# Writing the constant rows of four stacked operands on ScalarE instead of VectorE

## The chip, the cores and the metric

The kernel runs on one core of a Trainium2 chip. A core has TensorE (PE in the profile; its weight loads are shown as PEld), VectorE (DVE), ScalarE (ACT), GpSimd (POOL) and SyncE (SP), and each works through its own list of instructions in a fixed order. The metric is the device time of one execution in microseconds (us); less is better.

## The reference

Clustered attention feeds a routed mixture of experts, which feeds a dense layer pair with the mish activation:

```python
# 2 batches, 8 heads, 768 tokens, head size 64, 16 clusters
q_assign = argmax(normalize(q) @ normalize(centroids).T)   # k_assign alike
mask = q_assign[:, :, :, None] == k_assign[:, :, None, :]
scores = where(mask, scale * (q @ k.T), -1e9)
attn = exp(scores - scores.max(-1)); attn /= attn.sum(-1) + 1e-9
x = (attn @ v) as 1536 rows of 512
# 8 experts, one for each row: logits = x @ w_gate + modality_bias[modality_id]
x[e] = gate_w[e] * (relu(x[e] @ w1[e]) @ w2[e])
h = x @ w_in; g = h * tanh(softplus(h)); out = g @ w_out
```

## The kernel before, in words

There are 16 attention problems (2 batches of 8 heads). For each, the operands of the score product lie in one of four stacks, `QK[0]` to `QK[3]`, used in turn. A stack is a tile of 128 partitions and four planes (QA, QB, KA, KB) of 768 half-precision numbers. Partitions 0 to 95 hold high and low parts of q and k and arrive by four DMAs that `stack(i)` (L258 to L261) issues from SP's queue out of `hl`, where `split_pair` (L245 on ScalarE, L249 on VectorE or GpSimd) has put the high and the low part of a pair of heads. Partitions 96 to 127 carry the mask: in QA and KA the cluster of each token, written once for each head (L303, and for head 0 L332 and L334), in QB the running row maximum (L378, two of the rows), and in KB a constant that never changes: 65504 in partitions 96 and 97 and zero elsewhere. `shift_rows` writes the zeros of QB (L151, GpSimd) and then the constant rows of KB (L153), once for each of the four stacks. The constant comes from `frow`, a column that GpSimd builds (L146, L148).

At the start, the list of work is this. Four loads bring q and k of the first two pairs of heads; a fifth, from ScalarE's queue, brings the centroids `cen`. VectorE and ScalarE compute the norms of the centroids (L165 to L170, and in `centroid_stacks` two rounds of L175 to L177, then L178 and L179), VectorE scales the centroids (L181, L182), PE transposes them (L184, L185) and VectorE writes them as `CC` (L186 to L190). With `CC`, PE can compute the similarity of tokens and clusters, for head 0 from `hl` (L313) and for head 1 from its stack (L273). VectorE turns them into one-hot rows (L319 to L325, L286 to L292), and these go into the stacks. Then the scores of head 0 start: L350 and L355 for the row maxima, L391 for the scores themselves. `load_v` (L202) brings v of batch 0, which ScalarE scales (L221) before the split of v. ScalarE also copies the one-hot rows of head 1 (L301), which SP then sends into the stack (L303).

The function of the program that calls `shift_rows` asks for the rows of stack 0 early and for those of stacks 1 to 3 as steps that are interleaved with the main loop. The order that is written into each engine's list, though, is not this order: a planner puts the instructions of every engine but SP in order by its own estimate of times, and keeps dependencies. SP's list stays as written in the program. Each engine then follows its list and waits on semaphores.

After attention for batch 0 the expert phase begins to interleave with attention (`moe1`, L1007 and its neighbours), the weights of the dense layers are converted by VectorE and ScalarE (L1027 to L1035), and the dense layers follow (L1103 to L1164).

Of the kernel before, what the change touches and what calls it, by code (L numbers as in the profile page):

```python
# [13 lines left out]
AF = mybir.ActivationFunctionType  # L14
ALU = mybir.AluOpType
# [9 lines left out]
def clustered_attention_moe_kernel(  # L25
# [16 lines left out]
    nc = tc.nc  # L42
# [100 lines left out]
    QA, QB, KA, KB = range(4)  # L143
    QK = [ap.tile([P, 4, S], F16, name=f"QK{i}") for i in range(NST)]
    frow = ap.tile([P, 1], F32, name="frow")
# [4 lines left out]
    def shift_rows(i, eng):  # L150
        eng.memset(QK[i][96:128, QB, :], 0.0)  # L151
        yield
        nc.vector.tensor_scalar(out=QK[i][96:128, KB, :], in0=QK[i][96:128, QB, :], scalar1=frow[96:128], scalar2=None, op0=ALU.add)  # L153
        yield

    cen = a3.tile([P, S], F32, tag="e32", name="cen")[:, 0:P]
# [333 lines left out]
    def attention():  # L490
# [81 lines left out]
        assign_first()  # L572
        load_v(0, 0, T)
        run(shift_rows(0, nc.gpsimd))
        sk, sq = split_pair(1, 1, True), split_pair(1, 0, True)
        next(sk)
# [24 lines left out]
        for k_ in range(1, NST):  # L601
            put(start(shift_rows(k_, nc.gpsimd), 1), 1)
# [765 lines left out]
```

## Time and profile before

| | us |
|---|---|
| median of 3 runs | 689.66 |
| the three runs | 689.56, 689.66, 696.43 |
| the profiled execution | 697.58 |
| its span, first to last instruction | 695.9 |
| mean granted TensorE clock in it | 0.971 of full speed |

The profiled execution is one of its own, 7.92 us above the median, and 1.68 us of it lie outside the span. Rows of its trace give a start and a duration in us from the start of the span; in the timeline, brackets hold the time that the engine sat idle before the instruction and what released it.

### The profile page before, as it was taken

How to read it: one execution, taken by the hardware profiler on the slowest of the kernel's cores; microseconds unless marked ns; L12 is line 12 of the kernel's file. 1: busy time of each engine (PE TensorE's matmuls, PEld its weight loads, DVE VectorE, ACT ScalarE, POOL GpSimd, SP SyncE). 2: the span in 40 equal slices, each digit the busy share in tenths (PEclk: the TensorE clock that was granted, in tenths of full speed). 3: DMA queues.
4: the chain of work that ended last, by engine and by line, in shares of the span. 5: the costliest groups of instructions: out<-in, count | busy, mean ns of one | idle time of the engine just before them, and what ended most of it. 6: DMA issues, size and time to landing. Idle time of an engine off the chain costs nothing.

```text
span 695.9 us, 14026 instructions
## 1 busy us (share of the span) xinstructions
PE 616.7 (89%) x5618; PEld 409.6 (59%) x5619; DVE 400.6 (58%) x751; ACT 459.3 (66%) x699; POOL 294.9 (42%) x251
## 2 busy tenths in 40 slices
PE   1698999987589988987999889999999999999995
PEld 1365867756356645554766556666666667667542
DVE  6768767689699899999858888823121110110100
ACT  2587998875678767765677678846554476776500
POOL 5577888796776744551141211111311212313211
PEclk9999999989789999999999999999999999999999
DMA  7532372312853234346445544321100000000000
GB/s 229 139 74 64 87 206 53 87 41 61 273 162 102 68 97 121 123 128 189 135 158 183 183 150 161 113 61 31 47 16 1 15 16 1 31 1 31 2 31 34
DMA packets 56743, 64.43 MB, mean 93 GB/s; under 512 B 10080, under 2 KB 46944, under 8 KB 56672
## 3 DMA queue, kind: packets, MB, share of 16 engines
q1 hardware_dynamic: 42064, 48.74, 24.1%
q10 hardware_dynamic: 12688, 8.42, 4.0%
q0 software_dynamic: 1920, 6.32, 2.4%
q8 instruction: 46, 0.75, 0.5%
q14 instruction: 25, 0.20, 0.1%
HBM read 46.23 MB, written 6.32 MB: 76 GB/s over the span
## 4 chain that ended last, share of the span: by engine, by line
PE 40%; DVE 28%; issue 10%; ACT 9%; DMA 7%; SPq 3%; POOL 1%; ACTq 0%; POOLq 0%; DVEq 0%
PE h L1007 12%; PE o L1159 12%; PE eps L1007 6%; DVE f L1028 4%; DVE mxh L351 3%; DVE f L1030 3%; PE s L391 2%; DVE w L922 2%; DMA QK<-hl 2%; DVE f L1027 2%; DMA QK<-oT 2%; DVE win L1035 2%; DVE mxh L356 1%; DVE dg L702 1%; PE eps L273 1%
## 5 line engine op out<-in xcount | busy, mean ns | idle before, releaser
L114 POOL TENSOR_TENSOR el<-e,eh 128x768 f16<-128x768 f32 x86 | 146.0, 1709 | 63.9 <-ACT eh L400 42.9
L1007 PE MATMUL h<-x,win 128*128 128x256 f16 x1152 | 133.3, 273 | 3.2 <-ACT s L1103 2.4
L1007 PEld LDWEIGHTS <-win 128*128 128x128 f16 x1152 | 112.5, 98 | 24.1 <-issue 4.7
L1110 DVE SCALAR_TENSOR_TENSOR s<-s,h 128x1024 f32<-128x1024 f32 x24 | 29.3, 1222 | 167.4 <-ACT s L1108 164.8
L1007 PEld LDWEIGHTS <-w 128*128 128x128 f16 x768 | 75.2, 99 | 67.6 <-issue 12.1
L114 POOL TENSOR_TENSOR xb<-s,xb 128x1024 f16<-128x1024 f32 x18 | 39.6, 2201 | 142.7 <-ACT xb L1113 142.5
L1159 PE MATMUL o<-wout,xb 128*128 128x512 f16 x432 | 96.8, 379 | 0.0
L391 PE MATMUL s<-QK 128*128 128x384 f16 x320 | 80.2, 346 | 9.6 <-ACT e L393 9.2
L393 ACT ACTIVATE e<-s 128x384 f32<-128x384 f32 x152 | 70.0, 489 | 24.5 <-PE s L391 19.3
L1007 PE MATMUL eps<-xw,w 128*128 128x416 f16 x384 | 76.8, 349 | 8.7 <-DVE hT L969 3.2
L400 ACT ACTIVATE eh<-e 128x768 f16<-128x768 f32 x88 | 74.3, 848 | 2.5 <-PE s L391 1.3
L351 DVE TENSOR_REDUCE mxh<-x 128x1 f32<-128x512 f32 x96 | 64.6, 680 | 17.2 <-PE x L350 17.1
L1103 ACT ACTIVATE s<-h,cst 128x512 f32<-128x512 f32 x48 | 32.8, 686 | 61.8 <-PE h L1007 61.5
L1007 PE MATMUL eps<-hT,w 128*128 128x416 f16 x384 | 71.6, 339 | 0.7 <-DVE hT L969 0.7
L1159 PEld LDWEIGHTS <-xb 128*128 128x128 f16 x432 | 42.3, 98 | 47.6
L429 PE MATMUL av<-vst,el 128*128 128x65 f16 x528 | 61.3, 197 | 5.8 <-POOL el L114 5.8
L427 PE MATMUL av<-vst,eh 128*128 128x65 f16 x528 | 63.8, 198 | 1.9 <-DVE xt L442 1.6
L428 PE MATMUL av<-vst,eh 128*128 128x64 f16 x528 | 63.8, 199 | 0.0
L429 PEld LDWEIGHTS <-el 128*128 128x128 f16 x528 | 51.3, 102 | 15.5 <-POOL el L114 11.3
L427 PEld LDWEIGHTS <-eh 128*128 128x128 f16 x528 | 51.5, 100 | 9.1 <-DVE xt L442 2.6
L391 PEld LDWEIGHTS <-QK 128*128 128x128 f16 x384 | 35.3, 103 | 33.3 <-issue 20.6
L428 PEld LDWEIGHTS <-eh 128*128 128x128 f16 x528 | 51.4, 101 | 3.3 <-issue 0.3
(224 smaller groups left out, 1053.4 us busy)
## 6 DMA issues: line engine op xcount, KB each, us to landing
wf<-in_moe_w_dram ACTq DMA_DIRECT2D x16, 512.0 KB
raw<-in_moe_w_in_dram SPq DMA_DIRECT2D x16, 512.0 KB
raw<-in_moe_w_out_dram SPq DMA_DIRECT2D x16, 512.0 KB
wf<-in_moe_w_dram SPq DMA_DIRECT2D x16, 512.0 KB
QK<-hl SPq DMA_DIRECT2D x32, 192.0 KB
xs<-dr SPq DMA_DIRECT2D x12, 258.0 KB
t<-in_k_dram SPq DMA_DIRECT2D x8, 384.0 KB
t<-in_q_dram SPq DMA_DIRECT2D x8, 384.0 KB
```

The lines of the kernel that those rows point to most:

```text
L114: nc.gpsimd.tensor_tensor(out=out_, in0=in0, in1=in1, op=ALU.subtract)
L351: nc.vector.reduce_max(out=mx_t[i][:, t, 0:1], in_=sp, axis=AX.X)
L391: nc.tensor.matmul(sps[hf][:, 0:HS], lhsT=st[:, KA + a, kt * P:(kt + 1) * P], rhs=st[:, QA + a, hf * HS:(hf + 1) * HS], start=(a == 0), st ...
L393: nc.scalar.activation(out=e32[:, hf * HS:(hf + 1) * HS], in_=sps[hf][:, 0:HS], func=AF.Exp, scale=1.0 / float(D) ** 0.5)
L400: nc.scalar.activation(out=eh, in_=e32, func=AF.Copy)
L427: nc.tensor.matmul(av[:, t, :], lhsT=eh[:, cols], rhs=vs[:, h, 0:NV], start=(kt == 0 and t == 0), stop=False, skip_group_check=True)
L428: nc.tensor.matmul(av[:, t, 0:D], lhsT=eh[:, cols], rhs=vs[:, h, NV:], start=False, stop=False, skip_group_check=True)
L429: nc.tensor.matmul(av[:, t, :], lhsT=el[:, cols], rhs=vs[:, h, 0:NV], start=False, stop=(kt == T - 1), skip_group_check=True)
L1007: nc.tensor.matmul(out_, lhsT=wc[:, a, kk, ms], rhs=mv[:, c, kk, :], start=(i == 0), stop=(i == n - 1))
L1103: nc.scalar.activation(out=s[:, u:u + hf], in_=pt[:, u:u + hf], func=AF.Sigmoid, scale=2.0 ** -17, bias=cst[:, 1:2])
L1110: nc.vector.scalar_tensor_tensor(out=s, in0=s, scalar=2.0 ** -6, in1=pt, op0=ALU.mult, op1=ALU.mult)
L1159: nc.tensor.matmul(pts[t], lhsT=gsl[q % 2][f // FB][:, f % FB, a, t * P:(t + 1) * P], rhs=wout[:, c, f, :], start=(f == 0 and i_ == 0), st ...
```

## The change

The constant rows of each stack are no longer written by a VectorE `tensor_scalar` that adds `frow` to the zero rows, but by a ScalarE activation (Identity) with the same zero rows as input and `frow` as bias for each partition. There are four such instructions, 32 partitions by 768 half-precision numbers each.

```diff
     def shift_rows(i, eng):
         eng.memset(QK[i][96:128, QB, :], 0.0)
         yield
-        nc.vector.tensor_scalar(out=QK[i][96:128, KB, :], in0=QK[i][96:128, QB, :], scalar1=frow[96:128], scalar2=None, op0=ALU.add)
+        nc.scalar.activation(out=QK[i][96:128, KB, :], in_=QK[i][96:128, QB, :], func=AF.Identity, bias=frow[96:128])
         yield
```

## Rows read from the trace of the kernel before

**Rows 1.** The page's head: busy time of each engine.

```profile
PE 616.7 (89%) x5618; PEld 409.6 (59%) x5619; DVE 400.6 (58%) x751; ACT 459.3 (66%) x699; POOL 294.9 (42%) x251
```

**Rows 2.** Busy time by stretch; last columns: granted clock, DMA share, GB/s.

```profile
140.00:340.00 200.00, 165.51 (x1902) 110.35 (x1902) 182.87 (x331) 139.65 (x248) 117.34 (x90) 0.93 0.43 128
340.00:696.00 356.00, 340.00 (x2255) 217.16 (x2251) 120.84 (x198) 214.82 (x255) 75.42 (x50) 0.99 0.19 63
```

**Rows 3.** The chain that ended last, 7 to 25 us: start, duration, what.

```profile
7.33 4.01 DVE QK L153 x4
...
12.82 0.26 DVE cen L182
...
24.92 0.74 ACT oT L301
```

**Rows 4.** The four constant-row writes by line: duration in ns, min/median/max.

```profile
L153 DVE TENSOR_SCALAR QK<-QK,frow x4: 413/1016/1790, 7.3 to 10.9; 32x768 f16<-32x768 f16 x4
```

**Rows 5.** Timeline of GpSimd, 6 to 11 us.

```profile
6.24 0.18 POOL L148 TENSOR_SCALAR_AFFINE_SELECT frow<-frow 128x1 f32<-128x1 f32 x1
...
7.09 1.64 POOL L249 TENSOR_TENSOR hl<-t,hl 128x768 f16<-128x768 f32 x1 [0.67 <-ACT hl L245]
8.69 1.75 POOL L249 TENSOR_TENSOR hl<-t,hl 128x768 f16<-128x768 f32 x1
```

**Rows 6.** Timeline of VectorE, 7 to 13 us.

```profile
7.16 0.14 DVE L177 TENSOR_SCALAR cs<-cs 128x1 f32<-128x1 f32 x1
...
11.56 0.22 DVE L176 SCALAR_TENSOR_TENSOR cs<-cs 128x1 f32<-128x1 f32 x1
...
12.39 0.39 DVE L181 TENSOR_SCALAR cen<-cen,cs 128x32 f32<-128x32 f32 x2
```

**Rows 7.** Timeline of VectorE and GpSimd, later in attention.

```profile
166.75 1.64 POOL L114 TENSOR_TENSOR el<-e,eh 128x768 f16<-128x768 f32 x1 [0.43 <-PE av L429]
167.19 1.24 DVE L755 TENSOR_SCALAR gg<-gg 128x6 f32<-128x6 f32 x1
174.75 1.65 POOL L114 TENSOR_TENSOR el<-e,eh 128x768 f16<-128x768 f32 x1 [1.67 <-ACT eh L400]
174.92 1.50 DVE L810 SCALAR_TENSOR_TENSOR tab<-ge,gst 128x8 f32<-128x8 f32 x1
```

**Rows 8.** Timeline of ScalarE, 5 to 22 us.

```profile
5.41 2.54 ACT L245 ACTIVATE hl<-t 128x768 f16<-128x768 f32 x3
20.34 0.80 ACT L332 ACTIVATE QK<-x 32x768 f16<-32x768 f16 x1 [12.38 <-PE x L330]
21.16 1.15 ACT L221 ACTIVATE vf<-vf 128x512 f32<-128x512 f32 x2
```

**Rows 9.** Groups of ScalarE by shape: count, busy us, mean ns, idle before.

```profile
L1103 ACT ACTIVATE s<-h,cst 128x512 f32<-128x512 f32 x48 | 32.8, 686 | 61.8 <-PE h L1007 61.5
L1103 ACT ACT_TABLE_LOAD x24 | 30.8, 1283 | 2.5 <-PE h L1007 2.0
```

**Rows 10.** Timeline of PE, 15 to 25 us: similarities of heads 1 and 2.

```profile
15.88 1.26 PE L273 MATMUL eps<-CC,QK 96*128 96x16 f16 x24
23.84 0.85 PE L273 MATMUL eps<-CC,QK 96*128 96x16 f16 x15
```

**Rows 11.** DMA packets in 13.2:13.6, 18.5:19.0, 19.8:20.0 and 21.5:22 us, in that order.

```profile
DMA packets 15, 0.03 MB, mean 77 GB/s; under 512 B 0, under 2 KB 0, under 8 KB 15
DMA packets 67, 0.12 MB, mean 236 GB/s; under 512 B 11, under 2 KB 37, under 8 KB 67
DMA packets 31, 0.04 MB, mean 200 GB/s; under 512 B 6, under 2 KB 30, under 8 KB 31
DMA packets 7, 0.01 MB, mean 12 GB/s; under 512 B 3, under 2 KB 7, under 8 KB 7
```

**Rows 12.** Timeline of SP's queue: an issue of stack 0, the one of v.

```profile
6.66 0.66 SPq L259 DMA_DIRECT2D QK<-hl  x1
11.43 0.59 SPq L202 DMA_DIRECT2D vf<-in_v_dram  x1
```

## What the change should do to the time: the prediction

> **What bounds the kernel now.** I read the page first: PE is the busiest engine at 89% of the span, but no engine is full [rows 1]. The table by stretch says where each limit holds: between 140 and 340 us VectorE is busy 182.87 of 200 us and PE 165.51, and after 340 us PE is busy 340 of 356 us, ScalarE and VectorE far less [rows 2]. Neither stretch contains the changed instructions. They run once, early, so the third view is the chain of waits over the first 25 us. There all four constant-row writes stand on the chain, back to back, 4.01 us from 7.33 us on, between two rounds of the centroid norm: the norm goes on only when they end, at 11.34, and the scaled centroids that PE waits for are ready at 12.82 + 0.26 = 13.08 [rows 3]. The planner has hoisted all four of them in front of work that everything later needs. Whatever the start loses is lost for the whole kernel, because the loads of later heads, the expert phase and the dense layers are all released by work of the start; only the first loads run by themselves. So the question is how much of 4.01 us the start gives back.
>
> **What is removed.** The four writes took 413, 1016 and 1790 ns (least, median, longest) though their shape is the same [rows 4]. The timeline of GpSimd explains it: its two subtractions of the second pair run from 7.09 to 8.73 and from 8.69 to 10.44 [rows 5]. The first write starts at 7.33 and waits for the end of the first subtraction, the second for the end of the second; only the last two run at their own pace of 0.41 us. Thus 4 x 0.41 = 1.65 us are work and some 2.4 us are waiting for GpSimd. The waiting needn't go with the writes. What stands behind them on VectorE is the rest of the chain: L175, L176, L177, L178, L179, then two L181 and one L182, and some of these can be held in the same way. Later rows show which kinds: a `tensor_scalar` of 128x6 took 1.24 us and ended at 168.43 where GpSimd's subtraction ended at 168.39, and an L810 of the operation that L176 is took 1.50 us and ended at 176.42, GpSimd's at 176.40 [rows 7]. A 128x1 `tensor_scalar` such as L177 was not held: 0.14 us, within GpSimd's first subtraction [rows 5, 6].
>
> Sum for the new start. L175 (0.16 us) begins at 7.33 and L176 is due at 7.53. If it is held to 8.73, then L181, which begins 12.39 - 11.56 = 0.83 us after L176 [rows 6], is due at 9.56 and is held to 10.44. Held instructions ended 0.03 to 0.22 us behind GpSimd (the 0.22 is the first write's, 7.33 + 1.62 to 8.73), so the first L181 ends at 10.47 to 10.66. It ended at 12.39 + 0.24 = 12.63 before, and the scaled centroids came 0.45 us later; now they come at 10.9 to 11.1 instead of 13.08: 2.0 to 2.2 us gained. If L176, which has only one element in each partition, is not held, L181 is due at 7.53 + 0.83 = 8.36, the first one waits to 8.73, the second to 10.44, and the gain is 2.3 us. Either way the second subtraction stands in the path. If neither were held, the gain would be the whole 4.01 us.
>
> The Trainium skill has a rule for this that speaks against the change: its page "SBUF — State Buffer", section "SBUF: two separate sides", says that VectorE and GpSimd share one pair of ports as an exclusive lock, taken for the whole instruction, by a VectorE operation with two SBUF inputs or in a two-port mode against a GpSimd operation that reads SBUF. By that rule L176 is held as well, and the sum would be the lower one, 2.0 to 2.2 us; the rows of L755 and L810 agree with it [rows 7].
>
> **What of it reaches the end.** Next come PE's L313, then L273 for head 1, then VectorE's chain and ScalarE's L332. L273 began at 15.88 [rows 10] and needs stack 1 in place. Stack 1's short packets were over by 13.2 us, where only the 2 KB packets of v are left [rows 11], so a start at 13.8 is covered. L332 moves from 20.34 to about 18.2 and ends at 19.0. Behind it in ScalarE's order stands L221, which began at 21.16 [rows 8] and needs v. This load hides: it was issued at 11.43 [rows 12], nothing of the change moves that, and its last packets fall between 18.6 and 20.0 us (of the packets over 2 KB, some of which are stack 2's, 30 are left in 18.5 to 19.0 and one in 19.8 to 20.0) [rows 11]. So L221 can begin between 19.0 and 20.0, a gain of 1.2 to 2.1 us, and with it L301 at 24.92, which the chain passes through [rows 3]. Stack 2 is the other thing that becomes late: its last packets came after 21.5 us [rows 11], and head 2's similarities, at 23.84 in PE's order [rows 10], would move to about 21.8, when it has just landed. I take 1.8 us, with v complete at 19.4, the middle of its window.
>
> **What is added.** Four activations on ScalarE. The nearest row is L332 with the same shape and no bias, 0.80 us [rows 8]; the nearest with a bias for each partition is L1103, 686 ns for 512 elements, which scales to 1.03 us for 768 [rows 9]. So 3.2 to 4.1 us in all; I take 3.5, nearer to the same shape. ScalarE finishes its splits at 5.41 + 2.54 = 7.95 and sits idle for 12.38 us before L332 [rows 8]; about 10.2 us of that remain after the gain, and the rows are wanted only by the scores of head 0, past 20 us. So I cost them at nothing. If Identity made ScalarE load another table and the old one again, two loads of 1283 ns [rows 9] add 2.6 us, still under the cover. Without cover the price is 3.2 to 4.1 us of ScalarE, in front of whatever the planner puts behind them. No DMA is added or moved, and nothing waits on a new semaphore but ScalarE, for GpSimd's `frow`, done at 6.24 + 0.18 = 6.42 us [rows 5].
>
> **The sum.** The profiled execution would go from 697.58 to 695.8 us, its span from 695.9 to 694.1. That execution lies 7.92 us above the median of 689.66, which is nearer to what will be measured: 689.66 - 1.8 = 687.9 us, 0.3% less. About 1%, 6.9 us, is what a measurement of this kernel can tell from no change, since the three runs of the same program differ by 6.87 us.
>
> **Rivals.**
> *The whole 4.01 us* come back: 685.7. For it: the writes stand on the chain with all of it. Against it: the hold by GpSimd, then v and stack 2. It needs another order, with the splits of the second pair later. 7%.
> *Nothing:* the planner uses the freed slot for other VectorE work, such as a step of later heads, or v is what the start waits for. 689 to 690.5. 12%.
> *Slower, by ScalarE's order.* The four activations are put ahead of a split of the first pair. They can't start before `frow` is done at 6.4 us, so the split of q that began at 5.4 [rows 8] would begin at 6.4 + 3.2 = 9.6, 4.2 us later; SP's L259 waits for it, and every issue behind that in SP's list, v among them, moves from 6.66 to about 10.4, 3.7 us [rows 12]. v then lands past 22.7 us and L221 starts there instead of at 21.16: 1.5 to 2.5 us slower, 691.7. It decides from the point at which a constant row stands ahead of the second split in ScalarE's list. Against it: ScalarE has 12 free microseconds behind the splits. If they are put behind L332 instead, about 3.5 - 1.8 = 1.7 us are lost in front of L221, the same size. 10%.
> *The rest of the program falls elsewhere.* The planner orders four engines, and it has already carried these writes across the whole start; a start that is 1.8 us shorter can change orders later. And the granted clock, 0.93 of full speed between 140 and 340 us [rows 2], means that about 0.07 x 200 / 0.5 = 28 us of that stretch ran at the lower of PE's two clock levels, 1.2 GHz; the same program came out at 689.56 and at 696.43. I price this by that spread, 6.9 us to either side: 681 us with 16%, 695 to 698 us with 13%.
>
> **How the numbers follow.** The forecast itself, 687.6 to 688.5, has 42%. Faster by over 1% (under 682.8) comes from the last rival alone, 0.16. Slower by over 1% (over 696.6) from its other side, 0.13. The rest, 0.71, is within 1%: forecast, whole gain, nothing, and ScalarE's order. For 8 in 10 the range must go into both outer cases without holding them: 682 to 696.
>
> **What would show each step.** In the new trace no constant row stands on VectorE; four activations of 0.8 to 1.0 us stand on ScalarE between 7.9 and 18 us; L176 or an L181 is longer than 1 us while GpSimd subtracts; L182 ends at 10.8 to 11.1; L332 starts at 18 to 18.5; L221 starts at 19.0 to 20.0; the later stretches keep their order, 1.8 us earlier. The prediction is wrong if L182 comes before 10 us and the gain is carried on, if constant rows stand ahead of a split or right behind L332, or if the order of work in the stretch from 140 to 340 us is another.

## The result, and the profile of the changed kernel

| | before | changed |
|---|---|---|
| median of 19 runs each, us | 694.57 | 689.32 |
| lowest and highest, us | 688.81 to 698.62 | 683.86 to 696.07 |
| ratio | 1 | 0.9919, 95% interval 0.9893 to 0.9944 |
| profiled execution and span, us | 697.58, 695.9 | 687.57, 685.9 |
| mean granted clock in it | 0.971 | 0.975 |

The changed kernel is 0.8% faster: (1 - 0.9919) x 694.57 = 5.6 us, between 3.9 and 7.4. The ratio leaves out three disturbed runs of the changed kernel (695.69 to 696.07 us); the medians are those of all runs, and by them the gain is 694.57 - 689.32 = 5.25 us. The time forecast, 687.9 us, and the sign are right, the size of the change is not: 1.8 us were forecast from a base of 689.66 us, and 19 runs put that base at 694.57. The three runs shown in advance were a low draw, and that the time came out right is luck.

The start goes much as forecast, with two differences. The page's busy times say only that the writes moved: VectorE 395.8 us for 400.6, ScalarE 462.3 for 459.3 [rows 1].

```profile
PE 613.6 (89%) x5618; PEld 408.7 (60%) x5619; DVE 395.8 (58%) x747; ACT 462.3 (67%) x703; POOL 298.0 (43%) x251
```

The timeline of VectorE, 7.3 to 10.3 us (start, duration, what), answers to [rows 6]:

```profile
7.36 0.16 DVE L175 RECIPROCAL cs<-cs 128x1 f32<-128x1 f32 x1
7.56 1.38 DVE L176 SCALAR_TENSOR_TENSOR cs<-cs 128x1 f32<-128x1 f32 x1
...
9.54 0.39 DVE L181 TENSOR_SCALAR cen<-cen,cs 128x32 f32<-128x32 f32 x2
9.97 0.26 DVE L182 TENSOR_SCALAR cen<-cen,cs 128x64 f32<-128x64 f32 x1
```

and that of GpSimd to [rows 5]:

```profile
7.28 1.64 POOL L249 TENSOR_TENSOR hl<-t,hl 128x768 f16<-128x768 f32 x1 [0.86 <-ACT hl L245]
11.57 1.64 POOL L249 TENSOR_TENSOR hl<-t,hl 128x768 f16<-128x768 f32 x1 [2.65 <-ACT hl L245]
```

L176 took 1.38 us for 0.22 and ended at 8.94, GpSimd's subtraction at 8.92: held, as forecast. L175, a reciprocal of one input just ahead of it, went through beside GpSimd in 0.16 us. The two L181 took their 0.39 us and were not held, because the second subtraction didn't run beside them. It came at 11.57, after a wait for ScalarE. So L182 ended at 10.23, 2.85 us earlier than the 13.08 of before, not 2.0 to 2.2.

Why the second subtraction came late stands in the timeline of ScalarE, 7 to 25 us [rows 8]:

```profile
7.23 3.40 ACT L153 ACTIVATE QK<-QK,frow 32x768 f16<-32x768 f16 x4
10.65 0.84 ACT L245 ACTIVATE hl<-t 128x768 f16<-128x768 f32 x1
18.04 0.80 ACT L332 ACTIVATE QK<-x 32x768 f16<-32x768 f16 x1 [6.55 <-PE x L330]
20.55 1.15 ACT L221 ACTIVATE vf<-vf 128x512 f32<-128x512 f32 x2 [1.71 <-DMA vf<-in_v_dram]
...
23.69 0.85 ACT L301 ACTIVATE oT<-oC 128x384 f16<-128x384 f16 x1
```

The planner put the four writes ahead of the fourth split, not behind it. They take 3.40 us together, 0.85 from one to the next, with no table load between them. L332 starts at 18.04, 2.30 us earlier. Then ScalarE sits idle for 1.71 us, waiting for v, and L221 starts only 0.61 us earlier than the 21.16 of before. The chain of waits says the same: it is v, not VectorE, that ends the start now [rows 3]. Ahead of v it runs through SP's queue, where the issues of the stacks, back to back from 6.04 us on, stand in front of v's.

```profile
11.46 9.08 DMA vf<-in_v_dram
...
23.78 0.76 ACT oT L301
```

The issue of v is at its old place [rows 12], and it lands at 20.53. The packets of 20.0:20.2, 20.2:20.4 and 20.4:20.6 us show how late its large ones run (the last two figures are the packets under 2 KB and under 8 KB; their difference, 4, 3 and 0, is the packets over 2 KB):

```profile
DMA packets 31, 0.05 MB, mean 230 GB/s; under 512 B 5, under 2 KB 27, under 8 KB 31
DMA packets 25, 0.03 MB, mean 169 GB/s; under 512 B 6, under 2 KB 22, under 8 KB 25
DMA packets 28, 0.04 MB, mean 184 GB/s; under 512 B 4, under 2 KB 28, under 8 KB 28
```

Stacks 1 and 2 have become late too. In the timeline of PE, both heads' similarities now wait for a DMA of their stack, where before there was no wait [rows 10]. For stack 1 this is what turns the 2.85 us of L182 into the 2.30 of L332:

```profile
13.61 1.24 PE L273 MATMUL eps<-CC,QK 96*128 96x16 f16 x23 [0.28 <-DMA QK<-hl]
...
22.67 0.21 PE L273 MATMUL eps<-CC,QK 96*128 96x16 f16 x1 [0.83 <-DMA QK<-hl]
```

Of L301's gain of 1.13 us (24.82 to 23.69), 0.61 is L221's; the other 0.52 is an L222 that stood ahead of L301 and now stands behind it. That is a change of order, and it isn't the only one. From about 21 us to 450 us the lists of PE, VectorE, ScalarE and GpSimd are rearranged throughout: in PE's list, 5,571 instructions as it was recorded for the experiments below, 2,679 places hold another instruction, and a line-by-line comparison takes out or puts in 1,188. SP's list is the same. So the span's 10.0 us needn't come from the start. L440 runs once at the end of each of the 16 heads; its group, heads 0 to 6 and heads 7 to 15 (first and last start at the end of the row), of the kernel before:

```profile
L440 DVE TENSOR_SCALAR r<-av x7: 152/154/165, 54.7 to 133.1; 128x6 f32<-128x6 f32 x7
L440 DVE TENSOR_SCALAR r<-av x9: 149/152/157, 149.9 to 318.5; 128x6 f32<-128x6 f32 x9
```

and of the changed kernel:

```profile
L440 DVE TENSOR_SCALAR r<-av x7: 150/165/167, 51.6 to 132.0; 128x6 f32<-128x6 f32 x7
L440 DVE TENSOR_SCALAR r<-av x9: 147/151/165, 145.3 to 311.1; 128x6 f32<-128x6 f32 x9
```

The lead is 3.1 us at head 0, 1.1 at head 6, 4.6 at head 7 and 7.4 at head 15. A gain of the start that is handed on would stay what it is. The stretch from 140 to 340 us and the one after it answer to [rows 2] (columns as there):

```profile
140.00:340.00 200.00, 167.85 (x1935) 113.02 (x1934) 184.77 (x361) 143.74 (x251) 120.27 (x87) 0.95 0.45 131
340.00:686.00 346.00, 328.75 (x2174) 209.43 (x2172) 113.88 (x162) 207.18 (x247) 72.28 (x47) 0.99 0.19 63
```

In the 200 us every engine did slightly more work than before, VectorE 184.77 us for 182.87 and PE 167.85 for 165.51, and the granted clock was 0.95 for 0.93. No one resource stands out.

### The profile page after: what moved, and what is told of

Read it like the earlier page. It is cut to its first block, busy times and chain, and to the rows that moved or that the text cites. A ratio compares the mean times of both kernels' runs of the same rounds, so it can differ in the third digit from the quotient of the medians.

```text
span 685.9 us, 14017 instructions
## 1 busy us (share of the span) xinstructions
PE 613.6 (89%) x5618; PEld 408.7 (60%) x5619; DVE 395.8 (58%) x747; ACT 462.3 (67%) x703; POOL 298.0 (43%) x251
## 4 chain that ended last, share of the span: by engine, by line
PE 44%; DVE 23%; issue 10%; DMA 9%; ACT 9%; SPq 3%; POOL 1%; ACTq 0%; POOLq 0%; DVEq 0%
PE h L1007 13%; PE o L1159 12%; PE eps L1007 7%; DMA QK<-hl 3%; DVE f L1028 3%; DVE mxh L351 3%; PE s L391 3%; DVE f L1030 2%; DMA raw<-in_moe_w_out_dram 2%; DVE w L922 2%; DVE f L1027 2%; DVE win L1035 2%; DMA vf<-in_v_dram 1%; PE x L350 1%; PE av L425 1%
## 5 line engine op out<-in xcount | busy, mean ns | idle before, releaser
L114 POOL TENSOR_TENSOR el<-e,eh 128x768 f16<-128x768 f32 x86 | 149.5, 1750 | 53.2 <-ACT eh L400 39.8
L393 ACT ACTIVATE e<-s 128x384 f32<-128x384 f32 x152 | 69.1, 489 | 20.0 <-PE s L391 18.5
L1007 PE MATMUL eps<-xw,w 128*128 128x416 f16 x384 | 72.9, 339 | 4.9 <-DVE hT L969 3.4
```

What stands on the lines that cost most here:

```text
L114: nc.gpsimd.tensor_tensor(out=out_, in0=in0, in1=in1, op=ALU.subtract)
L393: nc.scalar.activation(out=e32[:, hf * HS:(hf + 1) * HS], in_=sps[hf][:, 0:HS], func=AF.Exp, scale=1.0 / float(D) ** 0.5)
L1007: nc.tensor.matmul(out_, lhsT=wc[:, a, kk, ms], rhs=mv[:, c, kk, :], start=(i == 0), stop=(i == n - 1))
```

## The experiments

Three theories. *Start:* the time comes back in the first 25 us, as forecast, whichever engine the writes leave VectorE's early place for. *Order:* most of it comes from the new lists that the planner made, and would come with the writes left where they were. *Engine:* it matters that ScalarE has the writes and VectorE hasn't.

To tell them apart, the order has to be held still while the writes move. In most kernels below each engine's list is therefore recorded from one planned program and fixed by dependencies that the planner obeys and that leave no instruction and no semaphore behind. Only a loop over leftover blocks, which isn't entered, can come out in another order. In the traces a and c run the four engines' instructions in before's order, the writes apart, and b in the changed kernel's. No kernel leaves out or changes part of the computation.

```diff
-        clustered_attention_moe_kernel(tc, *args)
+        clustered_attention_moe_kernel(tc, *args); _pin(tc, nc)
...
+            if prev is not None:
+                tc.add_manual_dep(nc.get_inst_by_name(f"I-{at}"), f"I-{prev}", info, reason="the recorded order")
```

All were timed in five rounds, on three chips. Ratios are to the kernel before on the same chip, whose medians there were 693.18, 693.15 and 693.95 us.

| kernel | writes on | lists | median us (runs) | ratio, 95% interval |
|---|---|---|---|---|
| a_act_old_order | ScalarE | before's | 691.96 (12) | 0.9972, 0.9942 to 1.0002 |
| b_dve_new_order | VectorE, old place | changed kernel's | 687.02 (6) | 0.9896, 0.9859 to 0.9933 |
| b2_dve_new_order | the same again | | 686.73 (11) | 0.9901, 0.9871 to 0.9930 |
| c_dve_late | VectorE, later | before's | 692.47 (12) | 0.9977, 0.9947 to 1.0006 |
| d_act_l301 | ScalarE | before's, L301 earlier | 690.89 (12) | 0.9956, 0.9929 to 0.9983 |
| h1_new_to128 | VectorE, old place | changed to 128 us, then before's | 691.02 (12) | 0.9961, 0.9932 to 0.9990 |
| h2_new_from128 | VectorE, old place | before's to 128 us, then changed | 689.70 (12) | 0.9960, 0.9927 to 0.9993 |
| f_new_l301 | ScalarE | changed, L301 earlier | 687.70 (12) | 0.9923, 0.9891 to 0.9955 |
| after_again | ScalarE | changed kernel as it is | 690.27 (12) | 0.9931, 0.9899 to 0.9964 |
| o_third_order | VectorE, old place | a third plan | 693.59 (12) | 0.9994, 0.9968 to 1.0021 |
| o_fourth_order | VectorE, old place | a fourth plan | 696.73 (12) | 1.0034, 1.0005 to 1.0062 |
| pool_writes | GpSimd | planner's own | 701.58 (7) | 1.0108, 1.0068 to 1.0148 |

**a_act_old_order: the edit alone.** The writes are on ScalarE at the place that the changed kernel gives them; every list is before's otherwise.

```diff
-        nc.vector.tensor_scalar(out=QK[i][96:128, KB, :], in0=QK[i][96:128, QB, :], scalar1=frow[96:128], scalar2=None, op0=ALU.add)
+        nc.scalar.activation(out=QK[i][96:128, KB, :], in_=QK[i][96:128, QB, :], func=AF.Identity, bias=frow[96:128])
```

> The four constant-row writes are on ScalarE, ahead of the last split as in the changed kernel, and every other instruction of every engine keeps the order of the kernel before. Start path plus new order (my theory): the start gains about 2.3 us up to L332, v holds L221 so that the gain behind it is 0.6 to 1.1 us, and the kernel is 0.5 to 2.5 us faster than before (ratio 0.9965 to 0.999). Start path alone: the whole of the measured 5.6 us is here, ratio about 0.992. New order alone: no change, ratio 1.000 within 0.0015.

Measured 0.9972: 1.9 us, with an interval from 4.0 faster to 0.1 slower. Its timeline of ScalarE:

```profile
18.05 0.80 ACT L332 ACTIVATE QK<-x 32x768 f16<-32x768 f16 x1 [6.73 <-PE x L330]
20.48 1.15 ACT L221 ACTIVATE vf<-vf 128x512 f32<-128x512 f32 x2 [1.63 <-DMA vf<-in_v_dram]
...
23.62 0.62 ACT L222 ACTIVATE vst<-vf 128x512 f16<-128x512 f32 x1
24.14 0.86 ACT L301 ACTIVATE oT<-oC 128x384 f16<-128x384 f16 x1
```

and its L440, heads 0 to 6 and 7 to 15:

```profile
L440 DVE TENSOR_SCALAR r<-av x7: 149/155/164, 54.1 to 132.3; 128x6 f32<-128x6 f32 x7
L440 DVE TENSOR_SCALAR r<-av x9: 148/151/165, 149.3 to 317.2; 128x6 f32<-128x6 f32 x9
```

L332 gains 2.29 us, v takes all but 0.68 of it away, and this remainder is handed on (the L222 ahead of L301, which the changed kernel has behind it, stands where it stood): 0.6, 0.8, 0.6 and 1.3 us at heads 0, 6, 7 and 15. This is what the edit does by itself in this order. The ratio alone doesn't show it, since its interval includes no gain, and two traces of one program can lie further apart (b and b2, next).

**b_dve_new_order and its repeat b2_dve_new_order: the order alone.** The writes stay on VectorE, at their old place behind L177; every list is the changed kernel's otherwise. Against the changed kernel:

```diff
-        nc.scalar.activation(out=QK[i][96:128, KB, :], in_=QK[i][96:128, QB, :], func=AF.Identity, bias=frow[96:128])
+        nc.vector.tensor_scalar(out=QK[i][96:128, KB, :], in0=QK[i][96:128, QB, :], scalar1=frow[96:128], scalar2=None, op0=ALU.add)
```

> The four writes stay on VectorE at their old place between the two norm rounds, and every other instruction of every engine has the order of the changed kernel. Start path plus new order: the norm ends at 13.1 us as before, and the kernel is 3 to 5 us faster than before (ratio 0.993 to 0.996). Start path alone: no change, 1.000 within 0.0015. New order alone: 0.992.

> The changed kernel's order with the writes left on VectorE, once more, since it had 6 runs and gave 0.9896. If the start's 2 us add to the order's gain, this must come out slower than the changed kernel (0.9919 and 0.9931): 0.994 to 0.997. If the new order has no use for a start that is earlier by 2 us: 0.990 to 0.993.

Measured 0.9896 and 0.9901: about 7 us, with nothing of the edit in it. The timeline of ScalarE of the first shows that the start is as late as before:

```profile
20.64 0.80 ACT L332 ACTIVATE QK<-x 32x768 f16<-32x768 f16 x1 [12.37 <-PE x L330]
...
24.61 0.85 ACT L301 ACTIVATE oT<-oC 128x384 f16<-128x384 f16 x1
```

and L440 that the lead comes after it:

```profile
L440 DVE TENSOR_SCALAR r<-av x7: 150/165/166, 53.6 to 132.7; 128x6 f32<-128x6 f32 x7
L440 DVE TENSOR_SCALAR r<-av x9: 147/150/165, 146.0 to 310.5; 128x6 f32<-128x6 f32 x9
```

The lead over the kernel before is 1.1 us at head 0, 0.4 at head 6, 3.9 at head 7 and 8.0 at head 15. The trace of b2, the same program, has

```profile
L440 DVE TENSOR_SCALAR r<-av x7: 152/165/167, 51.8 to 129.5; 128x6 f32<-128x6 f32 x7
L440 DVE TENSOR_SCALAR r<-av x9: 146/149/165, 142.8 to 306.9; 128x6 f32<-128x6 f32 x9
```

a lead of 2.9, 3.6, 7.1 and 11.6 us. Two executions of one program thus lie 1.8 us apart at head 0 and 3.6 at head 15, and a difference of that size between two traces shows nothing by itself. The changed kernel, with the better start and the same lists, is 2.0 us ahead of b at head 0 and 0.6 behind at head 15, and 0.2 ahead of b2 and 4.2 behind. The theory of the order stands, on the ratios; start and engine don't explain the result. The gain is larger than the 0.993 to 0.996 expected if start and order share it, and as large as the order alone was to give.

**c_dve_late: another place on the same engine.** In before's lists two of the writes go behind L182 and two behind the first L292.

```diff
 L177 TENSOR_SCALAR cs<-cs 128x1
-L153 TENSOR_SCALAR QK_117<-QK_117,frow 32x768
-L153 TENSOR_SCALAR QK_118<-QK_118,frow 32x768
-L153 TENSOR_SCALAR QK_119<-QK_119,frow 32x768
-L153 TENSOR_SCALAR QK_120<-QK_120,frow 32x768
...
 L182 TENSOR_SCALAR cen<-cen,cs 128x64
+L153 TENSOR_SCALAR QK_117<-QK_117,frow 32x768
+L153 TENSOR_SCALAR QK_118<-QK_118,frow 32x768
...
```

> The four writes stay on VectorE but later in its list, two behind L182 and two behind the first L292, where VectorE waits for PE; every other instruction keeps the order of the kernel before. If it is the place of the writes that costs and not their engine, L176 is held to 8.7 to 9.0 us, an L181 to 10.4 to 10.7, L182 ends at 10.9 to 11.1, and the kernel changes as much as with the writes on ScalarE in the old order (0.5 to 2.5 us faster by my theory). If VectorE's load as such counts, less than half of that.

Measured 0.9977, as a, and as there the interval includes no gain. In the traces the two come out alike, too: L221 waits for v in both and starts at 20.41 here, 0.75 us earlier than before, and at 20.48 in a. So nothing speaks for the engine, but v hides what difference there may be: L182 gains 1.94 us here (13.08 to 11.14) and 2.85 in the changed kernel. This kernel also keeps GpSimd's two subtractions back to back, 7.45 to 10.68 us, so its timeline of VectorE shows the second hold that the prediction had:

```profile
7.65 1.45 DVE L176 SCALAR_TENSOR_TENSOR cs<-cs 128x1 f32<-128x1 f32 x1
...
9.71 1.15 DVE L181 TENSOR_SCALAR cen<-cen,cs 128x32 f32<-128x32 f32 x2
10.89 0.25 DVE L182 TENSOR_SCALAR cen<-cen,cs 128x64 f32<-128x64 f32 x1
11.18 0.76 DVE L153 TENSOR_SCALAR QK<-QK,frow 32x768 f16<-32x768 f16 x2
```

The two L181 take 1.15 us for 0.39, and L182 ends at 11.14. The writes, held by nobody here, take 0.76 us for two.

**d_act_l301: v's wait taken out of L301's way.** As a, with L301 ahead of L221 in ScalarE's list.

```diff
 L332 ACTIVATE QK_117<-x 32x768
+L301 ACTIVATE oT<-oC 128x384
 L221 ACTIVATE vf<-vf 128x512 x2
...
-L301 ACTIVATE oT<-oC 128x384
```

> As the first kernel of this group (writes on ScalarE, old order), and in ScalarE's list the copy of head 1's one-hot rows, L301, moved ahead of the scaling of v, L221. If the load of v, through L221 in front of L301, is what stops the gain, L301 starts at about 20 instead of 24 us, SP's L303 with it, and the kernel is 1.5 to 4 us faster than the first kernel of this group. If something else is late next (stack 2, PE's row maxima), it is within 0.7 us of it.

Measured 0.9956: 3.0 us, between 1.2 and 4.9. The timeline of ScalarE, where L301 now goes at 20.23, and L221 behind it finds v there:

```profile
20.23 0.85 ACT L301 ACTIVATE oT<-oC 128x384 f16<-128x384 f16 x1 [1.30 <-DVE oC L299]
20.98 1.13 ACT L221 ACTIVATE vf<-vf 128x512 f32<-128x512 f32 x2
```

Its L440:

```profile
L440 DVE TENSOR_SCALAR r<-av x7: 149/155/165, 51.7 to 130.0; 128x6 f32<-128x6 f32 x7
L440 DVE TENSOR_SCALAR r<-av x9: 148/151/165, 145.9 to 314.1; 128x6 f32<-128x6 f32 x9
```

The lead is 3.0 us at head 0, 3.1 at head 6, 4.0 at head 7 and 4.4 at head 15. So with L301 out of v's way the start does hand on a gain in before's order, and v, through L221 and L301, is what stands in the way of it in kernel a. The expectation was 1.5 to 4 us ahead of a; by the medians it is 1.1, the intervals overlap, and the 2.4 us between their traces at head 0 are little more than the 1.8 between b and b2. That d beats a isn't shown.

**h1_new_to128 and h2_new_from128: which half of the new order.** The writes stay at their old place on VectorE, and the lists change over at about 128 us, from the changed kernel's to before's or the other way round. In terms of the lists:

```diff
-each engine: before's list
+each engine, h1: the changed kernel's list to 128 us, before's behind it
+each engine, h2: before's list to 128 us, the changed kernel's behind it
```

> The writes stay on VectorE at their old place; each engine has the changed kernel's order up to about 128 us and the old order behind it. Theory (the new order pays at the change of batch, 130 to 216 us): no change, ratio 0.998 to 1.001. Rival (it pays in the first 128 us and the rest only carries it on): 0.990 to 0.993. Rival (it is spread over the whole run): 0.995 to 0.997.

> The counterpart: old order up to about 128 us, the changed kernel's order behind it, writes on VectorE at their old place. Theory: 0.990 to 0.993, as with the whole new order. Rival (first 128 us): no change. Rival (spread): 0.995 to 0.997.

Measured 0.9961 and 0.9960, 2.7 and 2.8 us. Together they make 5.5 of the 7 us of kernel b, in equal parts as far as intervals of 0.7 to 4.7 and 0.5 to 5.1 us can tell. The idea that the new order pays at one place, the change from the first batch to the second, falls; it pays on both sides of the cut.

**f_new_l301 and after_again.** The first is the changed kernel with the same move of L301 as in d, the second the changed kernel once more.

```diff
 L332 ACTIVATE QK_117<-x 32x768
+L301 ACTIVATE oT<-oC 128x384
 L221 ACTIVATE vf<-vf 128x512 x2
...
-L301 ACTIVATE oT<-oC 128x384
```

> The changed kernel with its own order, except that on ScalarE L301 stands ahead of L221, which waits for v. If the start's gain adds to what the new order gives, and v in front of L301 limits the start here too: 1.5 to 3 us faster than the changed kernel, ratio to the kernel before about 0.988 to 0.990. If the new order has slack in which a start earlier by 2 us is lost: 0.990 to 0.993, as the changed kernel.

> The changed kernel itself, beside the others on the same chip, to place it against the writes on VectorE in the new order (ratio 0.9896). If the start's gain adds to the order's gain: 2 us under the kernel with the new order alone. If not: the same as that one, 0.988 to 0.993.

Measured 0.9923 and 0.9931. In the new order the move can't be seen in the time. No kernel fixes before's lists and leaves the writes in place, which would measure the fixing alone; but a, c and o_third (below) are fixed too and come out at 0.997 to 0.999, so fixing the lists isn't what gives b its 1%.

**o_third_order and o_fourth_order: other plans of the same work.** These run before's instructions with the lists that the planner makes when the writes are planned as two columns wide, and as plain fills. The code is before's; only the recorded lists differ, in 744 and 1,256 lines of PE's list by the comparison that gave 1,188 above.

```diff
-each engine: the list planned with 32x768 writes
+each engine, third: the list planned with 32x2 writes
+each engine, fourth: the list planned with fills in their place
```

> The work of the kernel before, to the instruction, the four writes at their old place on VectorE; but each engine has a third order, the one that the planner makes when the four writes are taken to be two columns wide. Theory (the planner's order moves this kernel by up to a per cent, whatever is changed): a ratio other than 1, between 0.990 and 1.010, of no foretold sign. Rival (the changed kernel's order is better for a reason that has to do with ScalarE and VectorE at the start): 1.000 within 0.002.

> As the third order, with a fourth: the one that the planner makes when the four writes are plain fills that can be done before the norm; the writes themselves are kept as before and at their old place. Same expectations: a ratio between 0.990 and 1.010 by the theory, 1.000 within 0.002 by the rival.

Measured 0.9994 and 1.0034. With b there are four plans of the same work now, from 1.0% faster to 0.3% slower. A different plan isn't a better one by itself. The third is within 0.002 of 1.000, where the rival that only the changed kernel's plan is better had put it; the fourth is not, but it is late from the start (L440 of head 0 at 57.8 us for 54.7). Three new plans are too few to say how often one is better.

**pool_writes: the writes on GpSimd.** The planner makes its own order.

```diff
-        nc.vector.tensor_scalar(out=QK[i][96:128, KB, :], in0=QK[i][96:128, QB, :], scalar1=frow[96:128], scalar2=None, op0=ALU.add)
+        nc.gpsimd.tensor_scalar(out=QK[i][96:128, KB, :], in0=QK[i][96:128, QB, :], scalar1=frow[96:128], scalar2=None, op0=ALU.add)
```

> The four writes on GpSimd, and the planner makes its own order. If leaving VectorE's chain is what counts: 0.991 to 0.995, as the changed kernel. If the order is a draw that each change makes anew, about 2 us from the start plus a draw: anywhere from 0.988 to 1.007.

Measured 1.0108, 7.5 us slower, outside both expectations. Its timeline of GpSimd:

```profile
7.31 6.84 POOL L153 TENSOR_SCALAR QK<-QK,frow 32x768 f16<-32x768 f16 x3
14.23 1.64 POOL L249 TENSOR_TENSOR hl<-t,hl 128x768 f16<-128x768 f32 x1
15.97 2.28 POOL L153 TENSOR_SCALAR QK<-QK,frow 32x768 f16<-32x768 f16 x1
18.34 1.64 POOL L249 TENSOR_TENSOR hl<-t,hl 128x768 f16<-128x768 f32 x1
```

and of VectorE:

```profile
7.46 0.76 DVE L176 SCALAR_TENSOR_TENSOR cs<-cs 128x1 f32<-128x1 f32 x1
...
8.83 0.76 DVE L181 TENSOR_SCALAR cen<-cen,cs 128x32 f32<-128x32 f32 x2
9.63 0.26 DVE L182 TENSOR_SCALAR cen<-cen,cs 128x64 f32<-128x64 f32 x1
...
20.45 0.36 DVE L292 TENSOR_TENSOR seq<-eps,smx 128x192 f32<-128x192 f32 x1 [2.87 <-POOL so L326]
```

L182 ends at 9.89, the earliest of all kernels, and it helps nothing: GpSimd spends 2.28 us on a write, its subtractions and then L326 come late, and VectorE waits 2.87 us for that at L292. How much of the 7.5 us is this and how much the new plan wasn't separated.

## Why the prediction was right in the start and wrong in size

- **Where the writes stood, and what was lost there:** right. They left the chain, and c shows that they can leave it without leaving VectorE.
- **L176 held by GpSimd:** right, 8.94 for 8.73 plus 0.03 to 0.22, in a run whose subtraction ended 0.19 us later than in the kernel before.
- **L181 held, L182 at 10.9 to 11.1:** wrong, 10.23, and the reason is in "What is added": the writes were expected behind ScalarE's splits, and the planner put them ahead of the fourth. That delayed GpSimd's second subtraction by 2.9 us (8.69 to 11.57), out of VectorE's way. Constant rows ahead of a split were one of the forecast's own signs of being wrong. Where the second subtraction stays, in c, the forecast holds: 11.14.
- **The Trainium skill's rule** (page "SBUF — State Buffer", section "SBUF: two separate sides") agrees with what L176 did here, 1.38 us for 0.22 beside a subtraction. Kernel pool_writes does not bear it out: there L176, with two inputs, started 0.15 us behind a GpSimd write and ended 1.3 us ahead of the write's end. Kernel c adds an L181 held beside the second subtraction.
- **Price and cover of the four activations:** right. 0.85 us each in a row for 0.80 to 1.03, 3.40 in all for 3.5, no table load, and ScalarE still idle for 6.55 us before L332.
- **L332 at 18.0 to 18.5:** right, 18.04, though by two misses that nearly cancel: L182 came earlier than forecast, and 0.55 us of that went at stack 1. In c, which has neither, it is 18.41.
- **L221 at 19.0 to 20.0, a gain of 1.8 us:** mis-sized. v landed at 20.53, not at 19.4, and the gain is 0.61 us (0.68 in kernel a). The term took the middle of a window of packets; but the engine waits for the last one, and [rows 11] had one of v's size as late as 19.8 to 20.0. In the changed kernel the large ones went on to 20.2 to 20.4, and the wait ended at 20.53.
- **Stacks 1 and 2:** stack 1 was called covered for a start of L273 at 13.8, and was: in c L273 starts at 13.96 and waits for nothing. In the changed kernel L273 is due earlier, because L182 is, and waits. Stack 2, called just in time for 21.8, keeps PE idle for 0.83 us, up to 22.67; the chain of waits does not pass there.
- **"The later stretches keep their order, 1.8 us earlier":** this step failed, and it decides the size; another order between 140 and 340 us was one of the forecast's own signs of being wrong. The forecast had the planner's new order as a rival with 16% on its faster side, priced at 6.9 us by the spread of the runs. That spread is of one program in one order, so it is luck that the price fits. Kernel b measures that rival alone at 0.9896 and 0.9901, about 7 us, and kernel a the forecast's mechanism alone at 0.9972. So a new order belonged in the forecast itself, and nothing in the trace of before could tell which way the order would fall: two other plans of the same work gave 0.9994 and 1.0034.
- **The base:** the forecast subtracted from a median of three runs. By the larger sample that was 4.9 us too low (694.57 - 689.66), and the gain 3.8 us too small (5.6 - 1.8). The time came out right because the two nearly cancel.

Two things stay open. The first is what in the new order pays. The halves give equal parts as far as can be told, and the clock of single profiled executions (kernel c's had 0.985 and a span of 687.0 us, while its ratio is 0.9977) hides a few us in comparisons of late stretches. Early on the traces do show one place. In before's list of ScalarE the first exponential of head 0 (L393) stands behind a split that waits 1.30 us for a load of k:

```profile
33.91 0.84 ACT L245 ACTIVATE hl<-t 128x768 f16<-128x768 f32 x1 [1.30 <-DMA t<-in_k_dram]
34.78 0.87 ACT L393 ACTIVATE e<-s 128x384 f32<-128x384 f32 x2
```

In b it stands ahead of it and starts 2.5 us earlier:

```profile
32.26 0.87 ACT L393 ACTIVATE e<-s 128x384 f32<-128x384 f32 x2
33.63 0.84 ACT L245 ACTIVATE hl<-t 128x768 f16<-128x768 f32 x1 [0.49 <-DMA t<-in_k_dram]
```

In b2 it starts at 32.31, in h1 at 32.05, in the changed kernel at 31.53; in the third plan, which keeps it behind the split, at 34.32. No kernel moves it alone, so what it is worth isn't shown.

The second is why the better start adds nothing in the new order: the changed kernel, at 0.9919 and 0.9931, isn't faster than b, at 0.9896 and 0.9901. Their intervals overlap, and a gain of the size of kernel a's, 1.9 us with an interval down to nothing, is about as much as these can tell. No kernel here clearly beats the changed one; the new order with the writes left on VectorE has the best ratios, and it shows that moving them is not what made the kernel faster.

## What to carry to other kernels

Before a gain on the chain is counted, look up what lands next, and take the last packet of that transfer, not the middle of its window: here v turned 2.3 us into 0.7. In a kernel whose lists are made by a planner, a small edit can also bring a new order, and three new orders of the same work were here worth between 1.0% faster and 0.3% slower; fix the lists before an edit gets the credit. And ask for the place of an instruction in its engine's list before its engine: four writes of 0.41 us took 4.01 us because they stood early and beside GpSimd's subtractions; leaving that place brought L182 forward by 1.94 us on VectorE and by 2.85 on ScalarE, and v left some 0.7 of either.

## What the runs showed of the hardware that was not expected

The same write of 32x768 half-precision numbers, with a value for each partition added, took 0.41 us on VectorE when nothing held it, 0.91 on ScalarE (0.85 from one to the next), and 2.20 to 2.28 on GpSimd. Beside the first of GpSimd's writes, which ran for 2.22 us from 7.31 to 9.53, L176 took 0.76 us and ended at 8.22: it was slowed, but not held to the end as beside a subtraction with two inputs. The two L181 beside the same write took 0.76 us for 0.39 and ended at 9.59, just behind it. What let L176 go earlier isn't shown. And v, issued at 11.46, landed 9.08 us later; before, no wait on it stood in the trace, so its lateness showed only in the packets.
